# A recurrent attention and a two-layer product on one core: the order of all steps written anew

## The chip, the core and the metric

The kernel runs on one core of one Trainium2 chip. The core has five engines that run side by side, each through its own list of instructions in order: TensorE (PE, matmuls, with weight loads as a second track), VectorE (DVE), ScalarE (ACT), GpSimd (POOL) and SyncE (SP, which here only issues DMAs). Matmuls write to PSUM, from which DVE and ACT can read. The metric is the device time of one execution in microseconds (us), smaller is better. Differences are told against the median of the runs.

## The reference

For each of 4 batches and 8 heads (768 tokens, head size 48) a state matrix is carried through the tokens, and the result is put through two matrix products with a clipped quadratic between them:

```python
for t in range(S):
    cur = einsum('bhd,bhe->bhde', u * k[t], v[t])
    y[t] = einsum('bhd,bhde->bhe', r[t], state + cur)
    state = w * state + einsum('bhd,bhe->bhde', k[t], v[t])
x = y as (3072 tokens, 384)
h = x @ w_in                       # 384 -> 2048
g = where(h >= 1, h, where(h <= -1, 0, (h + 1)**2 / 4))
out = g @ w_out                    # 2048 -> 384, float32
```

## The kernel before

**Tiling.** Tokens are taken in chunks of 128. A *unit* is one chunk of one batch, a *group* is a chunk of two batches, so there are 12 groups (0 to 11) of two units each; group g has the units 2g and 2g+1. Groups 0 and 1 (the first chunk of all four batches) are worked unit by unit, the others mostly as whole groups. The hidden layer of a group is worked in four *quarters* of 512 columns.

**Steps.** Every step is a small function `do_<name>`, and a string `ORDER` lists all steps one after the other. Reading it from left to right gives each engine its list; nothing else sets the order. A word such as `m0.1/1` means step m of group 0, quarter 1, in PSUM place 1; `Ks1.0=G` means step Ks of group 1, unit 0, on engine G (GpSimd; V is VectorE, A is ScalarE). In a word like `M3.12` the two digits behind the point are unit 1 and quarter 2. The steps:

- `LK`, `LR`, `LV` load k, r and v through SP's queue (line 253); `WI0` to `WI2` and `WO0` to `WO2` load the two weight matrices in pieces through POOL's queue (lines 244, 247).
- `ln`, `bw`, `bu`, `wq` bring the logarithm of w (`lwp`) and u (`up`) to all partitions with matmuls (lines 207, 211, 233). `Wup`, `Wdn` put the powers of w in PSUM (tiles up_t, dn_t), `WupS`, `WdnS` in SBUF, `uS` copies u to SBUF, `wE` and `wC` make the decay over a whole chunk.
- `Rs`, `Ks` scale r and k by powers of w, `KU` and `RKU` form u*k and r*u*k, `us` sums the latter per head (line 304), `V` casts v to bf16, `B` multiplies v by those sums (all of line 282, 112, 313).
- `TR`, `TK`, `T` transpose the scaled r and k on TensorE (line 330), `cR`, `cK`, `c` copy them out; from group 4 on DMA transposes on SP do it (`RT`, `KT`, line 318).
- `A`, `AA` are the scores (line 370), `AT` masks them (lines 379, 384, always DVE), `Y` multiplies them by v and adds the state's part (lines 432, 438), `y`, `yg` add B (lines 446, 450, always DVE).
- `Sp`, `Tm`, `decayg`, `sbf` carry the state (lines 405, 409, 413, 416).
- `X` and `xc` transpose y on TensorE for groups 0 to 2; from group 3 on `xcg` does it with a DMA transpose on SP (line 467). The result is the tile xT.
- `m` is a quarter of the first product (line 475, 12 matmuls into the tile hp). The clipped quadratic takes three steps: `r` (line 486 on ACT, or a clamp in line 483 on DVE), `s` (lines 493, 495, ACT), `g` (line 498, always DVE, which also reads hp).
- `M` is one unit and quarter of the second product (line 512, 4 matmuls into the tile op), `og`, `o`, `oA`, `oB` copy the sums out, `stg`, `st`, `stA`, `stB` store them. Unit 1 of group 11 is worked in two halves of 192 columns.
- `Z` issues idle matmuls on a zero tile, whose result nobody reads (line 566).

**PSUM.** The eight banks form two pairs (places 0 and 1 of `pair`) and, in the opening, four single banks (places 0 to 3 of `bank`). With the first pair of place 2 or 3 the single banks are given up and become two more pairs. A step that writes a place waits until the last reader of what stood there is done. All idle matmuls write one tile in pair 0, made once at the start by `Zs`.

The lines that a sentence can't say are the loop that turns the list into instructions and the copy of the last unit's halves, which both read one tile:

```python
for word in ORDER.split():
    ...
    steps[kind](e, [int(x) for x in banks], *args)

def half_out(e, g, j, i):
    copy(e, make("o", ("o", g, j, i), [P, UNITS, DO], F32)[:, 0, : DO // 2], tiles["op", g, j][:, i, : DO // 2])
```

Of the kernel before, what the change touches and what calls it, by code (L numbers as in the profile page):

```python
# [9 lines left out]
F32 = mybir.dt.float32  # L10
# [8 lines left out]
FG = 4  # L19
# [5 lines left out]
Zs/0 ln Z19 bw/1 LK0.0 bu/0 uS=V LK1.0 LR0.0 LK0.1 LR0.1 LV0.0 wq/2 WdnS Ks1.0=G LR1.0 LR1.1 Wdn/3 Ks0.0=V Ks0.1=V  # L25
TK0/0 Wup/1 Rs0.0=V TR0/3 LK1.1 cK0=A WupS KU0.1=G KU0.0=V RKU0.0=G cR0=A KU1.0=G LV0.1 Rs0.1=V Z2 TR1/1 A0/03 LV1.0
LV1.1 WI0 WI1 WI2 us0.0 cR1=A TK1/1 cK1=A AT0.1 Z4 A1/13 Rs1.0=V LR2.0 LR2.1 Rs1.1=V V0.1 AT1.0 V0.0 Z9 TR3/1 B0.0=G
AT1.1 RKU0.1=V wE AT0.0 wC=A us0.1 Z7 Y1/3 TR2/0 B0.1=G Y0/2 y0 y1 cR2=A RKU1.0=G Z8 X0/2 Z4 TK2/3 X1/0 Ks1.1=G xc0=A
Sp1/2 cK2=A xc1=A Z7 TK3/3 cK3=A Tm1 A2/20 m0.0/0 cR3=V us1.0 AT2.1 AT2.0 r0.0=A A3/31 AT3.1 KU1.1=G RKU1.1=G m0.1/1
V1.0 s0.0=A B1.0=G Sp2/2 AT3.0 us1.1 r0.1=A Tm2 Y2/3 y2 g0.0 V1.1 X2/0 LK2.0 Y3/1 B1.1=G s0.1=A LK2.1 Sp0/2 Sp3/3  # L30
xc2=V LK3 y3 WO0 WO1 m0.3/0 r0.3=A s0.3=A g0.1 X3/1 Tm0 xc3=V m0.2/1 LR3 LV2.0 Tm3 m1.1/2 g0.3 r1.1=V m1.0/3 m1.2/0
Ks2=G r0.2=A s0.2=A g0.2 sbf2=A s1.1=A r1.0=A s1.0=A sbf3=A g1.1 m1.3/1 r1.2=V WO2 KU2=G LV2.1 M0.00/2 M0.10 M0.11
M0.01 g1.0 M1.00/3 M1.10 M1.11 M1.01 Rs2=G s1.2=A g1.2 T5/0 RKU2=G LK4 r1.3=A s1.3=A g1.3 T4/1 LV3 Ks3=G M0.02 M0.03
LR4 us2 c5=V A5/0 KU3=G Rs3=G c4=V A4/1 AT5 sbf1=A M1.02 M0.12 M0.13 AT4 T6/0 sbf0=A V2 Y4/1 Y5 B2=G og0=A T7/2 c6=A
RKU3=G c7=A yg2 LV5 M1.12 Sp4/0 Sp5 M1.03 X5/2 Tmg2 decayg2=G X4/1 M1.13 A6/0 xc4=A xc5=V m2.0/2 A7/1 us3 AT6 m2.1/0
og1=A LK5 LR5 V3 Y6/3 B3=G sbfg2=A r2.0=A AT7 Y7 m2.2/1 s2.0=A Ks4=G yg3 xcg3 m2.3/3 g2.0 Rs4=G r2.1=A s2.1=A g2.1 LV4
# [574 lines left out]
```

## Time and profile before

| | before |
|---|---|
| median of 3 runs | 173.95 us (173.92 to 174.29) |
| profiled execution: span from its first to its last instruction | 172.6 us |
| TensorE busy in it | 164.4 us, 1674 matmuls |
| VectorE, ScalarE, GpSimd busy in it | 130.6, 129.9, 117.4 us |
| first matmul of m0.0, of m0.2 | 19.21, 27.27 us from the span's start |
| end of the last matmul | 169.14 us |

The span is one profiled execution, from its first to its last instruction; what lies around it, about 1.35 us, is the difference to the median of the timed runs. In the groups of the profile a row gives source line, engine, operation, output and inputs, shape and count, then busy time and mean duration in ns, then the engine's idle time just before and who ended it. In the timeline a row gives start and length in us. Tile names carry no numbers there.

### The profile page before, as it was taken

To read this page: it belongs to the slowest core of one execution; us is meant where nothing else is said; L and a number is where in the kernel's file an instruction comes from. 1 tells how busy PE (TensorE), PEld (TensorE's weight loads), DVE (VectorE), ACT (ScalarE), POOL (GpSimd) and SP (SyncE) were. 2 spreads that over 40 slices of the span, in tenths; PEclk is the share of its full clock that TensorE was granted. 3 is DMA by queue.
4 is the path that set the end of the run, shared out by engine and by line. 5 is a ranking of instruction groups with operands and counts; after the bars stand their busy time and mean duration, and the time that the engine had idled before them with its cause. 6 is when DMAs were issued, how large, how long until landed. Compare 5 with 4: busy or idle time off the path is not lost.

```text
span 172.6 us, 4051 instructions
## 1 busy us (share of the span) xinstructions
PE 164.4 (95%) x1674; PEld 132.9 (77%) x1674; DVE 130.6 (76%) x150; ACT 129.9 (75%) x150; POOL 117.4 (68%) x86
## 2 busy tenths in 40 slices
PE   7989968999999999989999999999999999999991
PEld 5769868966889777588787797696897787888871
DVE  4578698988687688859789779885889959873752
ACT  4355698991699899189979879689695896988940
POOL 3496744998689949999999998999568804300000
PEclk9999999999999999999999999999999999999999
DMA  6999999998996999999999997998999025140022
GB/s 114 194 184 179 199 187 180 228 210 174 206 191 99 206 184 168 194 199 145 196 312 210 182 220 163 223 182 155 297 170 267 4 52 145 37 104 0 8 91 91
DMA packets 103751, 28.26 MB, mean 164 GB/s; under 512 B 98866, under 2 KB 102836, under 8 KB 103732
## 3 DMA queue, kind: packets, MB, share of 16 engines
q1 hardware_dynamic: 101824, 24.75, 79.9%
q0 software_dynamic: 1760, 3.15, 9.8%
q8 instruction: 13, 0.21, 0.6%
q10 hardware_dynamic: 148, 0.10, 0.2%
q14 instruction: 6, 0.05, 0.1%
HBM read 20.45 MB, written 4.72 MB: 146 GB/s over the span
## 4 chain that ended last, share of the span: by engine, by line
PE 87%; ACT 4%; DMA 2%; DVE 2%; issue 1%; POOL 0%; ACTq 0%; DVEq 0%
PE hp L475 35%; PE op L512 34%; PE A L370 4%; PE Y L438 3%; DMA xT<-y 2%; PE Y L432 2%; PE Sp L405 2%; PE z L566 2%; ACT pt L486 1%; PE T L330 1%; ACT TT L112 1%; PE lwp L207 1%; PE wp L233 1%; PE TR L330 1%; PE TK L330 1%
## 5 line engine op out<-in xcount | busy, mean ns | idle before, releaser
L475 PE MATMUL hp<-xT,w_in 128*128 128x256 bf16 x576 | 69.1, 273 | 1.3 <-DMA xT<-y 0.8
L512 PE MATMUL op<-w_out,g 128*128 128x384 bf16 (+1 forms) x400 | 68.4, 320 | 0.0
L498 DVE SCALAR_TENSOR_TENSOR g<-sq,hp 128x1024 bf16<-128x1024 bf16 x48 | 57.9, 1215 | 13.2 <-ACT sq L495 13.2
L475 PEld LDWEIGHTS <-w_in 128*128 128x128 bf16 x576 | 61.9, 114 | 4.6 <-issue 1.6
L486 ACT ACTIVATE pt<-hp 128x1024 f32<-128x1024 f32 x46 | 46.9, 1021 | 13.7 <-PE hp L475 13.7
L512 PEld LDWEIGHTS <-g 128*128 128x128 bf16 x400 | 37.5, 98 | 20.4
L495 ACT ACTIVATE sq<-pt 128x1024 bf16<-128x1024 f32 x46 | 48.3, 1057 | 1.2
L379 DVE TENSOR_TENSOR AT<-A,umask 128x1024 bf16<-128x1024 f32 x20 | 23.7, 1220 | 5.2 <-PE A L370 5.2
L282 POOL TENSOR_TENSOR Ks<-Ki,Wdn 128x768 bf16<-128x768 f32 (+1 forms) x12 | 20.3, 1689 | 8.5 <-ACT Wdn L225 3.4
L313 POOL TENSOR_TENSOR V<-Vb,diag 128x768 f32<-128x768 bf16 (+1 forms) x14 | 18.1, 1291 | 9.8 <-DVE diag L304 4.4
L282 POOL TENSOR_TENSOR RKU<-Ri,KU 128x768 f32<-128x768 f32 (+1 forms) x13 | 21.2, 1630 | 1.1 <-DVE KU L282 0.7
L282 POOL TENSOR_TENSOR KU<-Ki,u_sb 128x768 f32<-128x768 f32 (+1 forms) x13 | 21.2, 1634 | 0.4 <-DMA Ki<-in_k_dram 0.4
L416 POOL TENSOR_TENSOR state<-Tm,wCm 128x768 f32<-128x768 f32 x8 | 14.6, 1824 | 9.8 <-DVE Tm L413 9.8
L282 POOL TENSOR_TENSOR Rs<-Ri,Wup 128x768 bf16<-128x768 f32 x10 | 18.2, 1820 | 0.3 <-DMA Ri<-in_r_dram 0.3
L112 ACT CAST Vb<-Vi 128x768 bf16<-128x768 f32 (+1 forms) x14 | 10.2, 733 | 5.4 <-DMA Vi<-in_v_dram 5.4
L450 DVE TENSOR_TENSOR y<-Y,V 128x768 bf16<-128x768 f32 x10 | 9.6, 956 | 5.9 <-PE Y L438 3.3
L304 DVE TENSOR_REDUCE diag<-RKU 128x16 f32<-128x768 f32 (+1 forms) x14 | 11.6, 831 | 1.5 <-POOL RKU L282 1.5
L112 ACT CAST state_bf<-state 128x768 bf16<-128x768 f32 (+1 forms) x12 | 8.5, 717 | 4.4 <-POOL state L416 4.4
L112 ACT COPY o<-op 128x768 f32<-128x768 f32 (+1 forms) x9 | 6.7, 748 | 6.0 <-PE op L512 5.9
L438 PE MATMUL Y<-Vb,AT 128*128 128x48 bf16 x192 | 10.4, 186 | 0.4 <-ACT Vb L112 0.4
L438 PEld LDWEIGHTS <-AT 128*128 128x128 bf16 x192 | 9.5, 98 | 0.7 <-issue 0.5
L413 DVE TENSOR_TENSOR Tm<-Sp,state 128x768 f32<-128x768 f32 x8 | 7.7, 956 | 3.1 <-PE Sp L405 3.1
(73 smaller groups left out, 123.3 us busy)
## 6 DMA issues: line engine op xcount, KB each, us to landing
out_dram<-o SPq DMA_DIRECT2D x11, 384.0 KB, 3.8
Ki<-in_k_dram SPq DMA_DIRECT2D x9, 384.0 KB, 6.2
Ri<-in_r_dram SPq DMA_DIRECT2D x9, 384.0 KB, 6.2
Vi<-in_v_dram SPq DMA_DIRECT2D x9, 384.0 KB, 5.4
Ki<-in_k_dram SPq DMA_DIRECT2D x6, 192.0 KB, 4.0
Ri<-in_r_dram SPq DMA_DIRECT2D x6, 192.0 KB, 4.7
Vi<-in_v_dram SPq DMA_DIRECT2D x6, 192.0 KB, 6.0
w_in<-in_moe_w_in_dram POOLq DMA_DIRECT2D x2, 384.0 KB, 7.5
```

The source lines that it names most:

```text
L112: nc.scalar.copy(out, in_) if e == "A" else engines[e].tensor_copy(out, in_)
L282: engines[e].tensor_mul(part(out)[:, :, :, :D], part(a), rep(b, j1 - j0) if len(b.shape) == 3 and b.shape[1] == H else part(b))
L304: nc.vector.tensor_reduce(d[:, hs], tiles["RKU", g][:, hs, :], AX.X, ALU.add)
L313: engines[e].tensor_mul(t[:, hs, :], tiles["V", g][:, hs, :], tiles["diag", g][:, hs].unsqueeze(2).to_broadcast([P, n, D]))
L379: nc.vector.tensor_mul(t.rearrange("p i n t -> p (i n) t"), tiles["A", n].rearrange("p i (n t) -> p (i n) t", t=P), umask.unsqueeze(1).to_ ...
L416: engines[e].tensor_mul(states[g % BP], tiles["Tm", g], flat(wCm).unsqueeze(1).to_broadcast([P, UNITS, DM]))
L438: nc.tensor.matmul(Y[:, h * D : (h + 1) * D], AT[:, i, p, :], V[:, j * H + h, :], start=(c == 0), stop=True, skip_group_check=True,)
L475: nc.tensor.matmul(hp[:, f, :], w_in_sb[wi][:, i, wo * FG * P + f : (wo + 1) * FG * P : FG], tiles["xT", g][:, :, i, :], start=(i == 0), s ...
L486: nc.scalar.activation(t, tiles["hp", g, q], AF.Relu, bias=0.5, scale=0.5)
L495: nc.scalar.activation(t, p, AF.Square)
L498: nc.vector.scalar_tensor_tensor(out=make("g", ("g", g, q), [P, FG, TOK], BF16), in0=tiles["sq", g, q], scalar=1.0, in1=tiles["hp", g, q], ...
L512: nc.tensor.matmul(tiles[key][:, i, : o1 - o0], tiles["g", g, q][:, f, j * P : (j + 1) * P], w_out_sb[wi][:, wo, f * DO + o0 : f * DO + o1 ...
```

## The change

The string `ORDER` is replaced as a whole. No step is added to or taken from the mathematics; their sequence changes, some move to another engine, and idle matmuls stand in other places (67 instead of 60, in nine bursts instead of eight, the first of 9 instead of 19). Three small changes of code go with it. An idle burst now takes a PSUM tile of its own (`Z` a single bank in the opening, `Zp` a pair). Each half of the last unit gets its own tile, so that a half's copy waits for that half alone, and which of its four quarters comes first is counted instead of fixed. `V` may run on another engine than ACT.

What moves between engines: to DVE two more KU, two more RKU (and two of half size), one Ks, one B, two decays, five more clamps `r`, half of a V cast, two half transposed copies and one whole; to POOL another half V cast; to ACT two more output copies of a group and the one of the last group's unit 0.

The diff, cut to its core (of `ORDER` two lines):

```diff
 ORDER = """
-Zs/0 ln Z19 bw/1 LK0.0 bu/0 uS=V LK1.0 LR0.0 LK0.1 LR0.1 LV0.0 wq/2 WdnS Ks1.0=G LR1.0 LR1.1 Wdn/3 Ks0.0=V Ks0.1=V
...
+ln=A LK1.1 LR0.0 LK0.0 Z9/0 bu/3 LK0.1 bw/1 Wup=A/0 Wdn=A/0 uS=V Rs0.0=V LR0.1 LK1.0 wq/3 Ks0.0=V LV0.0 LR1.1 KU0.1=V
...
     def do_V(e, b, g, j=None):
...
-        copy("A", t[:, hs, :], tiles["V32", g][:, hs, :])
+        copy(e or "A", t[:, hs, :], tiles["V32", g][:, hs, :])
...
-        key = ("op", g, j) if last else ("op", g)
-        if key not in tiles:
-            tiles[key] = pair(b[0], F32, "op")
         wi, wo = part(q, OUT_PARTS)
         for i, o0, o1 in [(i, i * DO // 2, (i + 1) * DO // 2) for i in halves] if last and j else [(j, 0, DO)]:
+            key = ("op", g, j, i) if last else ("op", g)
+            if key not in tiles:
+                tiles[key] = pair(b.pop(0), F32, "op")
+            n = counts["op", g, j, i] = counts.get(("op", g, j, i), 0) + 1
             for f in range(FG):
                 nc.tensor.matmul(
...
-                    start=(q == 0 and f == 0), stop=(q == nQ - 1 and f == FG - 1),
+                    start=(n == 1 and f == 0), stop=(n == nQ and f == FG - 1),
...
-        copy(e, make("o", ("o", g, j, i), [P, UNITS, DO], F32)[:, 0, : DO // 2], tiles["op", g, j][:, i, : DO // 2])
+        copy(e, make("o", ("o", g, j, i), [P, UNITS, DO], F32)[:, 0, : DO // 2], tiles["op", g, j, i][:, i, : DO // 2])
...
-    def do_Zs(e, b):
-        tiles["z"] = pair(b[0], F32, "z")
+    def idling(t, n):
+        for i in range(n):
+            nc.tensor.matmul(t, idle[:, :P], idle[:, :P], start=True, stop=True)
 
     def do_Z(e, b, n):
-        for i in range(n):
-            nc.tensor.matmul(tiles["z"][:, 0, :P], idle[:, :P], idle[:, :P], start=True, stop=True)
+        idling(pair(b[0], F32, "z")[:, 0, :P] if later else bank(b[0], [P, P], F32, "z"), n)
+
+    def do_Zp(e, b, n):
+        idling(pair(b[0], F32, "z")[:, 0, :P], n)
```

On DVE, from the first mask of group 1 to the second y of that group, the list before was this (AT_401 and AT_416 are the masked scores of units 3 and 2, state is the first state of a batch, y_458 the y tile of group 1):

```order
L384 TENSOR_TENSOR AT_401<-A1_376,umask_105 128x512
L384 TENSOR_TENSOR AT_401<-A0_375,umask_105 128x512
L384 TENSOR_TENSOR AT_416<-A1_407,umask_105 128x512
L384 TENSOR_TENSOR AT_416<-A0_406,umask_105 128x512
L304 TENSOR_REDUCE diag_399<-RKU_323 128x8
L409 TENSOR_TENSOR state_123<-Sp_439,wCm_110 128x384
L446 TENSOR_TENSOR y_458<-Y_449,V2_437 128x384
L498 SCALAR_TENSOR_TENSOR g_460<-sq_435,hp_385 128x1024
L112 COPY xT_492<-X_463 128x384
L446 TENSOR_TENSOR y_458<-Y_469,V2_437 128x384
```

And in the change (the two y of group 1 go to y_460):

```order
L387 TENSOR_TENSOR AT_387<-A1_356,umask_105 128x512
L387 TENSOR_TENSOR AT_387<-A0_355,umask_105 128x512
L285 TENSOR_TENSOR RKU_336<-Ri_166,KU_173 128x384
L387 TENSOR_TENSOR AT_427<-A0_391,umask_105 128x512
L412 TENSOR_TENSOR state_122<-Sp_401,wCm_110 128x384
L307 TENSOR_REDUCE diag_383<-RKU_336 128x8
L387 TENSOR_TENSOR AT_427<-A1_392,umask_105 128x512
L501 SCALAR_TENSOR_TENSOR g_458<-sq_412,hp_367 128x1024
L449 TENSOR_TENSOR y_460<-Y_432,V2_408 128x384
L115 CAST Vb_406<-Vi_259 128x384
L501 SCALAR_TENSOR_TENSOR g_466<-sq_464,hp_414 128x1024
L449 TENSOR_TENSOR y_460<-Y_495,V2_408 128x384
```

The second y now has a product RKU, a cast of half of V1 and a second g ahead of it; one transposed copy has moved behind it.

On POOL, the pieces of the first weight matrix stood together before, behind the first four products:

```order
L282 TENSOR_TENSOR Ks_91<-Ki_156,Wdn_114 128x8x48
L282 TENSOR_TENSOR KU_195<-Ki_151,u_sb_115 128x384
L282 TENSOR_TENSOR RKU_198<-Ri_158,KU_195 128x384
L282 TENSOR_TENSOR KU_201<-Ki_156,u_sb_115 128x384
L244 DMA w_in0_116<-in_moe_w_in_dram 128x3x512
L244 DMA w_in1_117<-in_moe_w_in_dram 128x3x512
L244 DMA w_in2_118<-in_moe_w_in_dram 128x3x1024
```

In the change:

```order
L285 TENSOR_TENSOR RKU_176<-Ri_131,KU_168 128x384
L247 DMA w_in0_116<-in_moe_w_in_dram 128x3x512
L285 TENSOR_TENSOR Ks_92<-Ki_129,Wdn_114 128x8x48
L247 DMA w_in1_117<-in_moe_w_in_dram 128x3x512
L285 TENSOR_TENSOR Ks_92<-Ki_129,Wdn_114 128x8x48
L316 TENSOR_TENSOR V2_280<-Vb_226,diag_183 128x384
L285 TENSOR_TENSOR KU_173<-Ki_129,u_sb_115 128x384
L316 TENSOR_TENSOR V2_280<-Vb_226,diag_183 128x384
L247 DMA w_in2_118<-in_moe_w_in_dram 128x3x1024
L115 CAST Vb_406<-Vi_259 128x384
```

w_in0 now comes behind three products, with a scaling of k between it and w_in1, and w_in2 behind four more steps.

On SP, what stands ahead of the first DMA transpose of y (group 3), before:

```order
L253 DMA Ki_677<-in_k_dram 128x16x48
L253 DMA Vi_694<-in_v_dram 128x16x48
L253 DMA Ri_705<-in_r_dram 128x16x48
L253 DMA Vi_809<-in_v_dram 128x16x48
L253 DMA Ki_896<-in_k_dram 128x16x48
L253 DMA Ri_898<-in_r_dram 128x16x48
L467 DMA_TRANSPOSE xT_952<-y_950 128x6x128
```

and in the change:

```order
L256 DMA Vi_658<-in_v_dram 128x16x48
L256 DMA Vi_693<-in_v_dram 128x16x48
L256 DMA Ri_695<-in_r_dram 128x16x48
L256 DMA Ki_697<-in_k_dram 128x16x48
L256 DMA Ri_699<-in_r_dram 128x16x48
L256 DMA Ki_701<-in_k_dram 128x16x48
L470 DMA_TRANSPOSE xT_962<-y_956 128x6x128
```

The six loads (k and r of groups 4 and 5, v of groups 3 and 4) are the same, in another sequence.

76 lines of the change are left out of this document (38 added, 38 removed).

## The prediction

> **What bounds the kernel now.** I read the page first: busy shares, the chain that ended last, the costliest groups.
>
> ```profile
> PE 164.4 (95%) x1674; PEld 132.9 (77%) x1674; DVE 130.6 (76%) x150; ACT 129.9 (75%) x150; POOL 117.4 (68%) x86
> ...
> PEclk9999999999999999999999999999999999999999
> ...
> PE 87%; ACT 4%; DMA 2%; DVE 2%; issue 1%; POOL 0%; ACTq 0%; DVEq 0%
> ...
> L498 DVE SCALAR_TENSOR_TENSOR g<-sq,hp 128x1024 bf16<-128x1024 bf16 x48 | 57.9, 1215 | 13.2 <-ACT sq L495 13.2
> L486 ACT ACTIVATE pt<-hp 128x1024 f32<-128x1024 f32 x46 | 46.9, 1021 | 13.7 <-PE hp L475 13.7
> L495 ACT ACTIVATE sq<-pt 128x1024 bf16<-128x1024 f32 x46 | 48.3, 1057 | 1.2
> ...
> Ki<-in_k_dram SPq DMA_DIRECT2D x6, 192.0 KB, 4.0
> ```
>
> TensorE is busy for 95% of the span and carries 87% of the chain, while DVE, ACT and POOL each have a quarter or more in hand. A quarter of the hidden layer costs 1.02 us (r) + 1.06 (s) + 1.22 (g) = 3.30 us behind its matmuls. Next, TensorE's waits, and two pieces of the chain in order of time (start, length, work).
>
> ```profile
> PE X L460 <- DVE y L446: 1.0, 1, 1.0
> PE hp L475 <- DMA xT<-y: 0.8, 1, 0.8
> PE hp L475 <- DVE g L498: 0.5, 1, 0.5
> PE Y L438 <- ACT Vb L112: 0.4, 1, 0.4
> ...
> 57.76 1.31 PE hp L475 x12
> 59.07 0.65 PE op L512 x4
> ...
> 68.81 0.96 DVE y L450
> 69.80 4.27 DMA xT<-y
> ```
>
> All waits but one lie before 27.3 us. The one behind is m4.0, which stands 0.8 us for its transposed input. From 27.27 us to the last matmul TensorE otherwise has work without a gap: a quarter (12 matmuls) takes 1.31 us, a step of the second product 0.65. Both kernels issue the same such work behind m0.2, and no idle burst stands there, so the order can gain in three places only: up to m0.2, at the 0.8 us, and after the last matmul.
>
> **The opening, up to the first quarter m0.0.** Times of the changed kernel are from here on my walk through its lists, with durations of these rows.
>
> ```profile
> 3.44 1.64 PE L207 MATMUL lwp<-lnw,ones 1*128 1x384 f32 x2 [0.24 <-ACT lnw L203]
> ...
> 4.88 1.48 PE L211 MATMUL up<-u_row,ones 1*128 1x384 f32 x2
> ...
> 7.80 0.61 PE L330 MATMUL TK<-ident,Ks 128*128 128x128 bf16 x4
> ...
> 10.08 0.61 PE L370 MATMUL A<-TT 48*128 48x128 bf16 x8
> ...
> 15.87 1.03 PE L566 MATMUL z<-idle 128*128 128x128 bf16 x8
> ...
> 16.15 1.02 DVE L446 TENSOR_TENSOR y<-Y,V 128x384 bf16<-128x384 f32 x2 [0.61 <-PE Y L438]
> ...
> 18.00 0.55 PE L566 MATMUL z<-idle 128*128 128x128 bf16 x7
> ...
> 19.21 1.50 PE L475 MATMUL hp<-xT,w_in 128*128 128x256 bf16 x12
> ```
>
> The up product now goes first. When u_row lands has no row; up ran at 4.88 straight behind lwp, so it was there by then. If it is there at 3.1 us (an estimate, a little before lwp's own start), up ends near 4.8 and lwp, which needs 1.3 us more, near 6.1 instead of 5.1. The exponentials move 1.0 us later, the copy of u into SBUF, which follows up (6.36 before), 1.5 us earlier. DVE now has Rs0.0 before Ks0.0, so Ks0.0 ends at 7.7 and TK0 starts at 7.8, as before: the swap costs nothing there. TR0 then stands behind four idle matmuls and needs PSUM bank 0, which holds dn_t until Ks0.1 has read it (8.7); A0 starts near 10.6 against 10.08. The two masks of unit 1 are done at 14.65, y0 at 15.15, y1 at 16.5 (before: both at 17.2), since DVE has fewer products of the later group in between. But X1, eight idle matmuls, TR2 and A3 stand ahead of m0.0 on TensorE: 17.05 + 0.35 + 0.8 + 0.45 + 0.45 gives m0.0 at 19.1. Against 19.21 that is no gain. Idle matmuls cost 0.13 us each at 15.9 us (1.03 for eight) and 0.08 at 18.0 (0.55 for seven, with the end of the last; some 0.06 from one start to the next), while the granted clock is 9 tenths or more in every slice. So with fast ones m0.0 comes at 18.7; with 0.5 us less luck at u_row and bank 0 it is 19.6. I take 19.1.
>
> **From m0.0 to m0.2.** This is the main term. DVE's list from the first mask of group 1 on, before:
>
> ```profile
> 19.53 1.28 DVE L384 TENSOR_TENSOR AT<-A,umask 128x512 bf16<-128x512 f32 x2
> 21.11 1.29 DVE L384 TENSOR_TENSOR AT<-A,umask 128x512 bf16<-128x512 f32 x2 [0.30 <-PE A L370]
> ...
> 22.78 0.55 DVE L409 TENSOR_TENSOR state<-Sp,wCm 128x384 f32<-128x384 f32 x1
> ...
> 23.73 1.21 DVE L498 SCALAR_TENSOR_TENSOR g<-sq,hp 128x1024 bf16<-128x1024 bf16 x1
> ...
> 25.53 0.56 DVE L446 TENSOR_TENSOR y<-Y,V 128x384 bf16<-128x384 f32 x1 [0.32 <-POOL V L313]
> 26.00 1.21 DVE L498 SCALAR_TENSOR_TENSOR g<-sq,hp 128x1024 bf16<-128x1024 bf16 x1
> ```
>
> The second y of group 1 ends at 26.1, with one g ahead of it. In the change a product RKU1.0, a cast of half of V1 and the second g stand ahead of it too. From 19.15 (A3 done): four masks 2.6, RKU1.0 0.5, state and reduction 1.0, g0.0 1.15, y 0.5, the cast 0.45, g0.1 1.15, y 0.55, total 7.9: the second y ends at 27.05, 0.95 later. (Each costs about 0.07 less than its row says, because the next begins before it ends. The cast of 128x384 on DVE has no row; it lies between the 0.35 of DVE's xT copy and the 0.56 of its f32 copy of u.)
>
> TensorE beside it, before:
>
> ```profile
> 22.54 0.36 PE L438 MATMUL Y<-Vb,AT 128*128 128x48 bf16 x8
> 23.87 0.34 PE L460 MATMUL X<-ident,y 128*128 128x128 bf16 x3 [0.97 <-DVE y L446]
> 24.64 0.36 PE L438 MATMUL Y<-Vb,AT 128*128 128x48 bf16 x8 [0.42 <-ACT Vb L112]
> 25.18 1.47 PE L475 MATMUL hp<-xT,w_in 128*128 128x256 bf16 x12
> 26.48 0.33 PE L460 MATMUL X<-ident,y 128*128 128x128 bf16 x3
> 27.27 6.73 PE L475 MATMUL hp<-xT,w_in 128*128 128x256 bf16 x60 [0.45 <-DVE g L498]
> ```
>
> From the first Y of group 1 to m0.2 that is 4.73 us, of which 1.84 are waits. In the change m0.1 ends at 22.75 and Y3 follows at 22.85; then come 9 idle matmuls (0.55), Sp3 (0.35), 22 idle ones (1.3), X3 0.3, Y2 0.35, m0.3 1.35, X2 0.3, Sp2 and Sp1 0.55: 5.45 us with Y3 itself. The 31 idle matmuls take the 1.85 us that were waits; the rest grew because Sp1, Sp2, Sp3 now lie here. m0.2 starts at 28.3 instead of 27.27: **+1.0 us**. The ends: idle matmuls at 0.13 us each add 2.1 (m0.2 at 30.4); an early m0.0 at 18.0 takes 1.1 off (27.2).
>
> **Loads and weights.** Two landings from the view of DMA issues (microseconds from issue to landing):
>
> ```profile
> Vi<-in_v_dram SPq DMA_DIRECT2D x1, 192.0 KB, 11.0
> ...
> w_in<-in_moe_w_in_dram POOLq DMA_DIRECT2D x1, 768.0 KB, 12.6
> ```
>
> While the three w_in transfers run, a 192 KB load takes 11 us; the median of the K halves on the page is 4.0. POOL now issues w_in0 near 9.3 us instead of 10.8, so the twelfth load, half of V1, lands near 24.9, just when DVE's cast wants it (24.95), and the eleventh near 21.8, in time for POOL's cast (1.0, as POOL's other 384-wide steps) and Y3. I cost both at nothing; the cover is a few tenths.
>
> **Behind m0.2.** DVE receives five clamps, two KU, two RKU, one Ks, one B, two decays and some copies, and gives up two output copies.
>
> ```profile
> L483 DVE TENSOR_SCALAR pt<-hp 128x1024 f32<-128x1024 f32 x2 | 2.4, 1220 | 0.0
> ```
>
> Five times 1.22, eight times 0.96 (the y row, same size) and 1.1 of smaller work: about 15 us, so DVE goes to 146 of 172.6 us. TensorE's list covers it: the shortest stretch between a quarter and the first user of its g or its PSUM pair is 3.7 us in both orders (a quarter 1.31, a mask product 0.55, a Y pair 0.75 and steps of 0.65), against the chain of 3.30. It costs nothing unless something queues ahead of r, s or g; both ends are priced below. Group 3's transposed load has the same six loads ahead of it on SP as before. For m4.0 the work between the last Y and the quarter grows from 4.45 to 4.79 us (two Sp more); need was 0.96 + 4.27 + 0.1. But g3.2 now stands directly ahead of that y on DVE, behind r3.2, a state copy and s3.2 on ACT, and I get the y 0.3 us later. I leave the 0.8 as it is; the ends are 0 and 1.2.
>
> **The tail.**
>
> ```profile
> 169.14 0.32 ACT L112 COPY o<-op 128x192 f32<-128x192 f32 x1 [3.13 <-PE op L512]
> 169.49 0.36 DVE L112 COPY o<-op 128x192 f32<-128x192 f32 x1 [0.45 <-ACT o L112]
> ```
>
> The two half copies came one after the other because they read one tile. With tiles of their own, the DVE half, now finished first on TensorE, is copied 0.35 us before the other half ends. But all three last stores now stand on SP, 0.34 us of issue each: the last issue ends about 1.05 us after the last matmul in both. Zero, between -0.3 and +0.2.
>
> **Sum.** Against the profiled span of 172.6: 0 (opening) + 1.0 (to m0.2) + 0 + 0 = 173.6. The median of the runs, 173.95, is 1.35 above that span, so the forecast is **174.9 us**, slower by 0.5%. Its own range is 174.3 to 175.8.
>
> **Rivals.** (a) *TensorE turns fast early.* If the idle matmuls between the opening's transposes bring it to the fast rate by about 11 us instead of 17, the 23 idle matmuls and five transposes between A0 and m0.0 cost half, m0.0 starts near 18.0 (when xT is there), and the 9.05 us of list behind it give m0.2 at 27.05: -0.2. If the y of group 4 is then on time too, the longer cover takes another 0.35: 173.4, faster. For it: idle matmuls now also lie between TK0, TR0 and A0. Against it: the opening burst shrinks from 19 to 9, and an idle matmul still took 0.13 us at 15.87, although the list of waits holds none above 1.0 us. The Trainium skill (TensorE: Matmul & The Clock Gate, Part 1) says that the array runs at half rate until about 3.4 us of sustained work; by that rule the changed opening is fast from 8 us and this rival's time follows, but the trace of before disagrees, being slow at 15.87. Chance 0.27.
>
> (b) *Half of V1 lands late.* If the w_in transfers hold their share without a gap, the twelfth load lands at 26.3 to 27.6; DVE's cast waits, and g0.1 and the second y with it, one for one beyond 24.95: 176.3 at the nearer end. Chance 0.13.
>
> (c) *DVE becomes the bound behind m0.2.* If the moved products stand ahead of g where only 0.4 us are spare (3.7 against 3.3), each such place costs some 0.3; six of the twelve groups make 1.8: 176.7. Against it: DVE's share stays at 85%. Chance 0.08.
>
> (d) *Nothing moves.* The walk's terms cancel and m0.2 starts where it did: 174.0. Chance 0.14.
>
> The forecast has 0.38. A difference under 0.2% (0.35 us) can't be told from none. Faster: 0.27, from (a). Same: 0.16, (d) and the low edge of the forecast. Slower: 0.57. The range runs from 172.9 (half a microsecond below (a)) to 177.0, above (c).
>
> **What would show it.** Right: first matmul of TK0 at 7.8, m0.0 near 19, the second y of group 1 behind both g's at about 27, an unbroken hp stretch from about 28.3, and the wait of m4.0 still near 0.8. Wrong: idle matmuls at 0.06 us before 12 us and the stretch before 27.3 (rival a); DVE waiting for a DMA before its cast (b); new TensorE waits on g or AT behind 28 us (c); a last store that ends more than 0.3 us nearer to the last matmul.

## The result

The change makes the kernel slower: the median is 176.69 us (four executions, 176.55 to 176.81) against 174.12 us of the kernel before in the same comparison, a ratio of 1.0133 (95% interval 1.0105 to 1.0162; the quotient of the two medians is 1.0148). Ratios here and below leave out executions that lie over 1.5% above the fastest of the same kernel. Forecast were 174.9 us, with 172.9 to 177.0 as range and 0.57 for slower. The sign held, and the time lies in the whole range, though above the 174.3 to 175.8 of the forecast itself. The reason did not hold: the forecast's one term, a microsecond between m0.0 and m0.2, did not come, and two places that it priced at nothing cost the time.

From here on lines of the changed kernel are the lines before plus 3. The page of the changed kernel, its first part and its clock row:

```profile
PE 165.3 (95%) x1681; PEld 132.7 (76%) x1681; DVE 147.8 (85%) x166; ACT 124.6 (71%) x143; POOL 103.8 (59%) x77
...
PEclk9999999999999999999999999999999999999999
```

DVE's share is where the forecast had it (146 us). TensorE's waits in the profiled execution:

```profile
PE Y L441 <- DVE AT L387: 2.6, 1, 2.6
PE up L214 <- DMA u_row<-in_u_dram: 1.0, 1, 1.0
PE z L566 <- DVE idle L137: 1.0, 1, 1.0
PE hp L478 <- DVE AT L382: 0.7, 1, 0.7
```

Two of these are new behind the start: 2.6 us for masks before Y0, and 0.7 us for masks before a quarter of the hidden layer. The 0.8 us for m4.0's transposed load is gone. Where the masks were late stands in the timeline of the changed kernel (start, length, engine, line, work):

```profile
8.41 1.00 POOL L285 TENSOR_TENSOR RKU<-Ri,KU 128x384 f32<-128x384 f32 x1 [1.02 <-DMA Ri<-in_r_dram]
8.55 1.28 DVE L285 TENSOR_TENSOR RKU<-Ri,KU 128x384 f32<-128x384 f32 x1
...
11.72 2.57 DVE L285 TENSOR_TENSOR Rs<-Ri,Wup 128x384 bf16<-128x384 f32 x1
12.07 1.01 POOL L285 TENSOR_TENSOR Ks<-Ki,Wdn 128x384 bf16<-128x384 f32 x1
13.03 0.83 POOL L316 TENSOR_TENSOR V<-Vb,diag 128x384 f32<-128x384 bf16 x1
13.81 1.32 POOL L285 TENSOR_TENSOR KU<-Ki,u_sb 128x384 f32<-128x384 f32 x1
14.67 1.87 DVE L387 TENSOR_TENSOR AT<-A,umask 128x512 bf16<-128x512 f32 x3
15.40 0.50 PE L441 MATMUL Y<-Vb,AT 128*128 128x48 bf16 x8 [2.58 <-DVE AT L387]
...
18.64 1.06 PE L566 MATMUL z<-idle 128*128 128x128 bf16 x8
...
20.60 1.50 PE L478 MATMUL hp<-xT,w_in 128*128 128x256 bf16 x12
...
28.71 1.47 PE L478 MATMUL hp<-xT,w_in 128*128 128x256 bf16 x12
...
109.23 1.80 POOL L285 TENSOR_TENSOR Ks<-Ki,Wdn 128x768 bf16<-128x768 f32 x1
109.49 2.36 DVE L285 TENSOR_TENSOR RKU<-Ri,KU 128x768 f32<-128x768 f32 x1
112.64 2.34 DVE L382 TENSOR_TENSOR AT<-A,umask 128x1024 bf16<-128x1024 f32 x2
113.90 1.47 PE L478 MATMUL hp<-xT,w_in 128*128 128x256 bf16 x12 [0.72 <-DVE AT L382]
```

A product of 128x384 costs DVE 0.55 us. Rs1.1 took 2.57, and it ended 0.43 us behind the end of POOL's B0.0 (13.86 to 14.29). RKU0.0 took 1.28 and ended 0.42 us behind POOL's RKU0.1 (9.41). RKU9, of 128x768, took 2.36 instead of 0.95 and ended 0.82 behind POOL's Ks9. All three read both of their inputs from SBUF, and each ends behind a POOL step by about its own running time. Before, DVE had four such steps, and none began while a POOL product ran. In the change it has fourteen. Five of them met a POOL product and took longer than others of their size: these three (Rs1.1 began 0.35 us ahead of the product that went first), B3 at 53.01 (1.40) and KU11 at 126.09 (1.30). A sixth, at 61.40, began 0.03 us before a product's end and took 0.95. The groups of Rs1.0 and Rs1.1 show it as well, before and after:

```profile
L282 DVE TENSOR_TENSOR Rs<-Ri,Wup 128x384 bf16<-128x384 f32 x2 | 1.0, 550 | 0.0
...
L285 DVE TENSOR_TENSOR Rs<-Ri,Wup 128x384 bf16<-128x384 f32 x2 | 3.1, 1559 | 0.0
```

Where the span's 2.3 us (172.6 to 174.9) lie:

| from to | before | after | difference |
|---|---|---|---|
| start to m0.0 | 19.21 | 20.60 | +1.39 |
| m0.0 to m0.2 | 8.06 | 8.11 | +0.05 |
| m0.2 to the start of m11.3 | 135.12 | 135.87 | +0.75 |
| m11.3 to the end of the span | 10.19 | 10.29 | +0.10 |

Outside the span nothing changed. The four executions of the changed kernel have 1.75 to 1.81 us there, and the 67 of the kernel before that were timed beside the experiments have 1.72 to 1.85. The 1.35 us of the forecast came from setting the median time against the span of an execution that was longer than the median one.

### The profile page after: what moved, and what is told of

It reads as the page before. It is cut to its first block, busy times and chain, and to the rows that moved or that the text cites. A ratio compares the mean times of both kernels' runs of the same rounds, so it can differ in the third digit from the quotient of the medians.

```text
span 174.9 us, 4046 instructions
## 1 busy us (share of the span) xinstructions
PE 165.3 (95%) x1681; PEld 132.7 (76%) x1681; DVE 147.8 (85%) x166; ACT 124.6 (71%) x143; POOL 103.8 (59%) x77
## 5 line engine op out<-in xcount | busy, mean ns | idle before, releaser
L489 ACT ACTIVATE pt<-hp 128x1024 f32<-128x1024 f32 x41 | 41.9, 1021 | 18.7 <-PE hp L478 17.6
L498 ACT ACTIVATE sq<-pt 128x1024 bf16<-128x1024 f32 x41 | 43.3, 1058 | 1.2
L316 POOL TENSOR_TENSOR V<-Vb,diag 128x768 f32<-128x768 bf16 (+1 forms) x13 | 16.6, 1276 | 25.6 <-ACT Vb L115 11.1
L285 POOL TENSOR_TENSOR KU<-Ki,u_sb 128x768 f32<-128x768 f32 (+1 forms) x11 | 18.6, 1691 | 3.2 <-DVE u_sb L115 3.1
L285 POOL TENSOR_TENSOR Ks<-Ki,Wdn 128x768 bf16<-128x768 f32 (+1 forms) x11 | 18.4, 1677 | 1.3 <-PE Sp L408 1.2
L285 POOL TENSOR_TENSOR RKU<-Ri,KU 128x768 f32<-128x768 f32 (+1 forms) x9 | 16.3, 1814 | 1.0 <-DMA Ri<-in_r_dram 1.0
L115 ACT COPY o<-op 128x768 f32<-128x768 f32 (+2 forms) x12 | 8.7, 728 | 8.7 <-PE op L515 8.7
L419 POOL TENSOR_TENSOR state<-Tm,wCm 128x768 f32<-128x768 f32 x6 | 11.0, 1830 | 5.7 <-DVE Tm L416 5.7
L441 PE MATMUL Y<-Vb,AT 128*128 128x48 bf16 x192 | 10.6, 186 | 2.6 <-DVE AT L387 2.6
L496 ACT ACTIVATE sq<-pt 128x1024 bf16<-128x1024 f32 x7 | 7.4, 1055 | 3.0 <-DVE pt L486 3.0
L115 ACT CAST Vb<-Vi 128x768 bf16<-128x768 f32 (+1 forms) x12 | 9.1, 773 | 0.5 <-DMA Vi<-in_v_dram 0.5
```

The costliest lines, as they stand in the source:

```text
L115: nc.scalar.copy(out, in_) if e == "A" else engines[e].tensor_copy(out, in_)
L285: engines[e].tensor_mul(part(out)[:, :, :, :D], part(a), rep(b, j1 - j0) if len(b.shape) == 3 and b.shape[1] == H else part(b))
L316: engines[e].tensor_mul(t[:, hs, :], tiles["V", g][:, hs, :], tiles["diag", g][:, hs].unsqueeze(2).to_broadcast([P, n, D]))
L441: nc.tensor.matmul(Y[:, h * D : (h + 1) * D], AT[:, i, p, :], V[:, j * H + h, :], start=(c == 0), stop=True, skip_group_check=True,)
L489: nc.scalar.activation(t, tiles["hp", g, q], AF.Relu, bias=0.5, scale=0.5)
L498: nc.scalar.activation(t, p, AF.Square)
```

## The experiments

Theory (*port*): a DVE step with two SBUF inputs that meets a running POOL product stands still till POOL is done, and the loss follows from three such meetings. The Trainium skill has this as a rule (SBUF — State Buffer, Who interferes with whom): such a step and a POOL instruction that reads SBUF share one read interface, and the one that comes second is blocked for the whole of the other. Rivals: late data; the list behind m0.0; the loads.

**Rs1.1 from PSUM.** The same values stand in the PSUM tile up_t, so one input can come from there with the order unchanged.

```diff
-        t = tiles["up_t"] if g == 0 and "up_t" in tiles else flat(Wup)
+        t = tiles["up_t"] if (g == 0 or (g, j) == (1, 1)) and "up_t" in tiles else flat(Wup)
```

> The changed kernel, in which Rs1.1 alone reads the powers of w from the PSUM tile up_t instead of from the SBUF tile Wup (the same values; order and all else stay). Theory (port): a DVE step with two SBUF inputs that meets a running POOL product stands still until that product ends; with one input in PSUM it does not. Rs1.1 then takes 0.55 us instead of 2.57 and ends near 12.3, Y0's wait of 2.6 us falls below 1.0, y0 ends near 15.2 instead of 17.0, and m0.0 starts at 18.6 to 19.3 instead of 20.60, since POOL's B0.1 and the transposes stand behind it still. m0.2 then starts near 27.3 instead of 28.71, and the time is 175.0 to 175.6 us. Rival (late data): Rs1.1 stood because r of unit 3 was not there; then it ends at 14.3 again and the time stays at 176.7. Rival (idle matmuls or DVE's list behind m0.0 set m0.2): Rs1.1 gets short, but m0.2 stays at 28.3 or later, and the time at 176.2 to 176.7.

One execution took 175.28 us, the other three 183.71 to 185.65; the profiled one is of the long kind. Its timeline:

```profile
11.96 0.55 DVE L285 TENSOR_TENSOR Rs<-Ri,up_t 128x384 bf16<-128x384 f32 x1
...
18.67 1.50 PE L478 MATMUL hp<-xT,w_in 128*128 128x256 bf16 x12
...
26.80 3.40 PE L478 MATMUL hp<-xT,w_in 128*128 128x256 bf16 x29
...
50.91 1.82 POOL L285 TENSOR_TENSOR Ks<-Ki,Wdn 128x768 bf16<-128x768 f32 x1
51.18 9.42 DVE L316 TENSOR_TENSOR V<-Vb,diag 128x768 f32<-128x768 bf16 x1
...
57.99 1.79 POOL L285 TENSOR_TENSOR Ks<-Ki,Wdn 128x768 bf16<-128x768 f32 x1
...
61.72 2.72 PE L478 MATMUL hp<-xT,w_in 128*128 128x256 bf16 x12 [7.96 <-DVE y L453]
```

Rs1.1 took 0.55 us, m0.0 came at 18.67 and m0.2 at 26.80, 1.9 us sooner: late data and the list behind m0.0 fall as causes of that loss. RKU0.0 still met POOL and took 1.11 us, so its meeting is not what held m0.0. The port theory is borne out for Rs1.1 by an edit that moved one operand and nothing else. What nobody expected is B3, the product that the change had moved to DVE: it met five POOL products in a row and stood till the last of them was over (59.78; it ended 0.82 later, 9.42 us in all). TensorE waited 7.96 us for it. In the profiled execution of the changed kernel the same B3 came 0.6 us before the end of one product, was let in behind it, and took 1.40.

**RKU9 on POOL.**

```diff
-RKU9=V
+RKU9=G
```

> The changed kernel, with RKU9 back on POOL (the place in the list stays). Theory (port): RKU9 on DVE (109.49, 2.36 us) makes two masks of group 8 late, and they alone cause the 0.72 us in which TensorE waits before m7.0 (113.90); without it that wait goes, 176.0 us, give or take 0.2. Rival: POOL gets 1.8 us more ahead of Ks9 and B8, so that y of group 8 and its transposed load come late and a wait takes the place of the one removed: 176.5 to 177.0.

175.29 us, ratio 1.0079 (1.0040 to 1.0117). Five of the eight executions took 174.85 to 175.44, three 176.25 to 176.91, about as long as the changed kernel. In the profiled one (175.15) the 0.72 us wait is gone; m7.0 there:

```profile
112.68 1.47 PE L478 MATMUL hp<-xT,w_in 128*128 128x256 bf16 x12
```

From m0.2 to m11.3 it took 134.69 instead of 135.87. The two traces agree to 0.02 us from m0.2 to m7.1 and from m7.3 to m11.3; between m7.1 (108.41 in the changed kernel) and m7.3 it took 8.31 instead of 9.47, so RKU9 on DVE cost 1.2 us, more than the one wait that the list shows for it, while KU11, further down, ran in 0.95 instead of 1.30 without any gain. The edit takes the whole product off DVE, not its stall alone; but at 0.95 us the first mask would have ended near 112.5, before m7.0 was due at 113.2 (an estimate from the rows of the changed kernel). The rival (a late B8) falls for this execution; what made three executions longer is open.

**Both edits**, as the two diffs above show them.

> Both edits at once. Theory (port): they add, since one lies before 28 us and one at 110: 174.2 to 174.9 us. If all of the loss against the kernel before came from steps that stood still beside POOL, it is within 0.3 us of 174.1. Rival: the list behind m0.0 (idle matmuls, second g and product ahead of the second y) costs its 1.0 us as the prediction has it; then it is 175 or more.

The executions took 173.56 and 173.74; 175.05 to 175.34 (three); 183.41 to 185.48 (five); none lies in the expected 174.2 to 174.9. Without the last group the ratio is 1.0015 (0.9982 to 1.0047). The profiled one (173.74), one of the two short ones, has m0.0 at 18.50, m0.2 at 26.82, m11.3 at 161.71 and a span of 172.0: 2.9 us less than the change, 0.6 less than before. In it the two edits take away more than the whole loss in the span; the rival, the list's 1.0 us, falls.

**The cost by itself.** A tail behind the kernel before runs DVE steps alone and beside POOL products:

```diff
+    def pool_products(n):
+        for i in range(n):
+            nc.gpsimd.tensor_mul(gb, ga, ga)
+    def two_sbuf():
+        for i in range(6):
+            nc.vector.tensor_mul(dx, flat(Wup), flat(u_sb))
...
+    two_sbuf()
...
+    pool_products(4)
+    two_sbuf()
...
+    pool_products(4)
+    for i in range(6):
+        nc.vector.tensor_add(dx, ps, flat(u_sb))
...
+    pool_products(4)
+    for i in range(6):
+        nc.vector.tensor_copy(db, flat(u_sb))
...
+    for i in range(3):
+        nc.gpsimd.dma_start(out=w_in_sb[0], in_=w_in_src[:, :, : FG * P])
+    two_sbuf()
```

> The kernel before, with a tail behind its last copy that measures the disputed cost by itself: six DVE steps of 128x384 at a time, alone or beside four POOL products of 128x768 (f32, 1.8 us each). Theory (port): six DVE products with two SBUF inputs take 2.9 us alone (0.48 each); beside POOL each waits for the POOL product that runs, so the six take 7 us or more, and POOL's products also get longer by about 0.5 each. Six DVE additions with one PSUM input stay at 2.9 beside POOL. Beside three DMA issues on POOL the two-input products stay at 2.9. Rival (POOL slows all that DVE does): the additions with a PSUM input get longer too. The six plain casts from f32 to bf16 (one SBUF input, 0.35 each) aren't decided by the theory as told; with them short, the number of SBUF inputs is what counts.

One step of each part, in that order, and for the second part also two of POOL's products:

```profile
172.38 0.56 DVE L604 TENSOR_TENSOR Wdn<-Wup,u_sb 128x384 f32<-128x384 f32 x1
...
184.26 1.66 POOL L600 TENSOR_TENSOR state<-state 128x768 f32<-128x768 f32 x1
184.62 1.70 DVE L604 TENSOR_TENSOR Wdn<-Wup,u_sb 128x384 f32<-128x384 f32 x1
185.99 1.66 POOL L600 TENSOR_TENSOR state<-state 128x768 f32<-128x768 f32 x1
...
191.53 0.56 DVE L616 TENSOR_TENSOR Wdn<-ps,u_sb 128x384 f32<-128x384 f32 x1
...
199.46 1.51 DVE L620 CAST state_bf<-u_sb 128x384 bf16<-128x384 f32 x1
...
205.38 3.52 DVE L604 TENSOR_TENSOR Wdn<-Wup,u_sb 128x384 f32<-128x384 f32 x6
```

Two SBUF inputs: 0.56 alone, 1.70 beside POOL, whose products took 1.66 there instead of 1.47. One input in PSUM: 0.56 beside POOL. Beside DMA issues: six in 3.52, as alone (3.52); only the first of the three issues ran at the same time. The open point came out against "two inputs alone count": a plain cast within SBUF, 0.36 alone, took 1.51. The Trainium skill (same page and section) names casts among the steps that can take both interfaces; this trace agrees. The rival (POOL slows all that DVE does) falls with the PSUM row.

**B3 on POOL too.**

```diff
-B3=V
+B3=G
```

> The changed kernel with three edits: Rs1.1 reads up_t in PSUM, RKU9 is back on POOL, and B3 is back on POOL (its place in the list stays). With the first two alone the time fell into groups (173.6 to 173.7, 175.1 to 175.3 and 183.4 to 185.5 us), and in a traced execution of the long kind B3 on DVE took 9.42 us, over five POOL products in a row (51.18 to 60.60). Theory (port): which group comes depends only on whether B3 gets its turn behind the first, or only behind the last of these five products; with B3 on POOL the groups are gone and every time is 173.4 to 174.0 us, 0.2 to 0.5 below the kernel before. Rival (another cause, for instance the granted clock or the loads): times above 175 come again. Rival: POOL, 1.5 us longer in front of Rs4, makes y of group 3 and its transposed load late: one group, but 174.3 or more.

174.05 us (173.45 to 175.15), ratio 0.9987 (0.9962 to 1.0013). None of ten executions is above 175.2, and none of the 52 of the later kernels with this edit is above 176.4: the 183 to 186 us were B3's. The rest of the expectation fails: three of ten still lie at 174.77 to 175.15, so B3 was not the only cause of spread, and the ratio's interval contains 1: with three edits the new order is as fast as the old one, not faster.

**Rs1.0 ahead of RKU1.1**, on top of the three edits.

```diff
-RKU1.1=V Rs1.0=V
+Rs1.0=V RKU1.1=V
```

> The same with Rs1.0 ahead of RKU1.1 on DVE. In the trace with two edits the two stood beside POOL's cast of half of V1 (0.79 and 0.85 us instead of 0.55), and TensorE waited 0.67 us before the transposes TR2, which need Rs1.0. Theory (port, and the opening sets m0.2): that wait falls below 0.2, m0.0 starts near 18.0 instead of 18.5, m0.2 near 26.3, and the time is 0.3 to 0.6 us below that of the kernel with three edits: 172.9 to 173.6. Rival (the loads or the second y set m0.2): m0.2 stays at 26.8 and the time is the same within 0.2.

174.06 us, ratio 0.9996 (0.9966 to 1.0026): the rival is right. m0.0 stands at 18.53 (18.66 with three edits) and m0.2 at 26.81 (26.77). The wait of 0.67 us that the edit was to remove is not in the trace with three edits either.

**Without the 31 idle matmuls** Z9 and Z22, on top of the three edits.

```diff
-Y3/2 Z9/1 Sp3/3
+Y3/2 Sp3/3
...
-Z22/0 X3/1
+X3/1
```

> The kernel with three edits without the 31 idle matmuls between Y3 and X3 (Z9 and Z22). The step of the prediction that put m0.2 one microsecond later rests on DVE's list, with these idle matmuls only in the place of waits. Theory (that step): TensorE waits there for y instead; m0.2 and the time stay as in the kernel with three edits within 0.2 us. Rival (they stand in the way): the time falls by 0.3 or more. Rival (they keep TensorE at its fast rate): the matmuls behind them get slow (X3 near 0.5 instead of 0.34, the quarter m0.3 above 1.5), and the time grows by 0.3 or more.

175.31 us, ratio 1.0067 (1.0043 to 1.0092), with two executions at 173.58 and 173.72 and six at 175.19 to 176.04. The profiled one is of 173.72:

```profile
24.15 0.34 PE L463 MATMUL X<-ident,y 128*128 128x128 bf16 x3 [1.25 <-DVE y L449]
24.42 0.37 PE L441 MATMUL Y<-Vb,AT 128*128 128x48 bf16 x8
24.97 1.50 PE L478 MATMUL hp<-xT,w_in 128*128 128x256 bf16 x12 [0.18 <-DMA w_in<-in_moe_w_in_dram]
```

X3 waits for y instead and runs at the fast rate (0.34), and m0.2 starts at 26.81: in this execution idle matmuls neither cost nor give anything there. The quarter m0.3 waits 0.18 us for w_in2, so a load stands close behind. The times don't bear the first theory out: most executions are about 1.5 us longer, and why this trace can't say.

**The load of w_in2 sooner**, on top of the three edits.

```diff
-B0.0=G TR3/2 KU1.0=G B0.1=G y0=V WI2
+B0.0=G TR3/2 B0.1=G WI2 KU1.0=G y0=V
```

> The changed kernel with Rs1.1 from PSUM, RKU9 and B3 on POOL, and three neighbours on POOL in another order: B0.0, B0.1, the load of w_in2, KU1.0 instead of B0.0, KU1.0, B0.1, w_in2. In the traces with three edits the load of w_in2 was issued at 15.6 to 15.8 and landed 9.1 to 9.2 us later, at 24.9, where the quarter m0.3 stood at 24.85 to 24.97, with a wait of 0.18 for that load in one of them; and y1 waited for POOL's B0.1. Theory (loads): with the stalls beside POOL gone, w_in2 sets m0.3 and with it m0.2. Issued near 14.4 it lands near 23.6; y1 ends 0.3 to 0.6 earlier, m0.0 starts near 18.1, m0.3 near 24.3, m0.2 near 26.2, and the time is 173.0 to 173.5 us, 0.4 to 0.7% below the kernel before. If the times of 174.8 to 175.5, which came in 3 of 10 and 6 of 8 executions, are those in which w_in2 lands later, they become rare. Rival (the second y of group 1 sets m0.2): within 0.2 us of the kernel with three edits.

174.16 us, ratio 0.9999 (0.9975 to 1.0023). In the profiled execution (174.10) the load was issued 1.0 us sooner than with three edits (14.65 instead of 15.64) but landed only 0.3 sooner, m0.2 came 0.11 sooner (26.66), and the gain went in two places:

```profile
15.48 1.01 POOL L285 TENSOR_TENSOR KU<-Ki,u_sb 128x384 f32<-128x384 f32 x1
16.19 1.17 DVE L285 TENSOR_TENSOR RKU<-Ri,KU 128x384 f32<-128x384 f32 x1
16.43 0.50 POOL L115 CAST Vb<-Vi 128x384 bf16<-128x384 f32 x1
...
38.96 1.46 PE L515 MATMUL op<-w_out,g 128*128 128x384 bf16 x8 [0.49 <-DMA w_out<-in_moe_w_out_dram]
```

KU1.0, now later on POOL, holds up RKU1.1, which also has to let POOL's cast pass (m0.0 stays at 18.54), and TensorE now waits 0.49 for a piece of w_out.

**The last stores apart**, on top of that.

```diff
-st11.0 stA11.1 stB11.1
+st11.0 stB11.1 stA11.1=A
```

> The same, and at the end the last half's store on ACT's queue and behind the other half's, which is ready first. In the trace with three edits the halves were copied by 168.32 and 168.60, and SP issued both stores from 168.63 on, 0.85 us together. Expected: the last issue ends 0.3 to 0.5 us sooner, and the time is 0.2 to 0.5 us lower than with the four edits. Rival (the landing of the last store counts from its copy, and the queue is not the limit): the same time within 0.1.

174.33 us, ratio 1.0001 (0.9981 to 1.0021). From m11.3 to the end of the span it took 10.20 us against 10.26: the rival is right, the queue is not the limit. But the profiled execution is a long one (175.58), and it shows one way in which an execution gets long. Its timeline:

```profile
123.89 1.82 POOL L285 TENSOR_TENSOR RKU<-Ri,KU 128x768 f32<-128x768 f32 x1
123.95 2.57 DVE L285 TENSOR_TENSOR KU<-Ki,u_sb 128x768 f32<-128x768 f32 x1
...
127.71 2.78 PE L478 MATMUL hp<-xT,w_in 128*128 128x256 bf16 x24 [1.16 <-DVE g L501]
```

The same place with three edits (173.59 us):

```profile
123.31 1.04 DVE L285 TENSOR_TENSOR KU<-Ki,u_sb 128x768 f32<-128x768 f32 x1
...
123.49 2.55 POOL L285 TENSOR_TENSOR RKU<-Ri,KU 128x768 f32<-128x768 f32 x1
```

KU11 on DVE and RKU10 on POOL meet. With three edits KU11 begins 0.18 us ahead of RKU10, while POOL's Rs10 still runs (to 123.52); it is let in behind Rs10 and ends in 1.04, and RKU10 is the one that stands (2.55 instead of 1.82), which TensorE doesn't wait for. In the long execution KU11 begins 0.06 us behind RKU10 and takes 2.57, g comes late, and TensorE waits 1.16.

**The order with four edits, without idle matmuls**: w_in2 sooner, the old stores, and Z9 and Z22 taken out by the diff shown for them above.

> The four edits, without the 31 idle matmuls Z9 and Z22. With three edits the kernel without them had the same m0.2 (26.81 against 26.77), but 6 of 8 executions took 175.2 to 176.0 us instead of 173.6 to 173.7. Theory (late w_in2): w_in2 issued 1.2 us sooner takes these away, and the times are those of the kernel with four edits, within 0.2. Rival (idle matmuls hold something up that the traced executions didn't show, such as the granted clock): most executions again take 1.5 us more than the shortest.

174.79 us (173.37 to 176.36), ratio 1.0008 (0.9972 to 1.0044): w_in2 was not the cause of the long executions. Six of ten took 174.7 or more, about as the rival has it, against two of the twelve with the idle matmuls; with three edits it was six of eight against three of ten. So kernels without these idle matmuls are long more often, and no run shows why. The profiled one, 174.87, has KU11 at 2.05 us and a wait of 0.6 for g. So of six profiled executions with B3 on POOL the four at 173.6 to 174.1 have KU11 at 0.95 to 1.04, and the two at 174.9 and 175.6 have it at 2.05 and 2.57. That KU11 makes the spread is read from these six traces and not shown; the kernel with KU11 on POOL as well, which should show it and should lie near 173.6 in every execution, was not tried.

**When is DVE let in?** Two tails of eight trials each: POOL does five products in a row, DVE one product of 128x768, which comes 0 to 7 short copies later.

```diff
+    for n in range(8):
...
+        for o in outs:
+            nc.gpsimd.tensor_mul(o, ins, dve_in[0])
+        for i in range(n):
+            nc.vector.tensor_copy(small[:, :144], ps[:, :144])
+        nc.vector.tensor_mul(dve_out, dve_in[0], dve_in[1])
```

In the second tail the five products are Ks, KU, Rs, KU, Ks, and DVE's is B.

> The kernel before, with a tail behind its last copy: eight times POOL does five independent products of 128x768 (f32, 1.8 us each) in a row, and DVE one product of the same size with two SBUF inputs, which comes 0, 1, 2, ... 7 short copies (one PSUM input, about 0.22 us each) after POOL's first has begun. The question is what decides whether DVE gets its turn behind the first POOL product or only behind the last. Theory (late comers win): in the traces DVE won where it came 0.5 to 0.7 us before the end of a POOL product (rows 53.01, 126.09) and lost over five where it came 1.55 us before it (51.18); then the first trials last 8 us or more and those that come in the last 0.7 us last 1.4 to 1.7. Rival (turn by turn, as the repeated short products showed: 1.61 to 1.71 each): no trial lasts longer than one POOL product and its own 0.95, 2.8 us.

> The kernel before, with a tail behind its last copy: the eight trials again, with the very kinds of step that met in group 2: on POOL Ks, KU, Rs, KU, Ks (128x768, Rs and Ks to bf16 in rows of 64), on DVE the product B (v in bf16 times one number per head). With plain f32 products DVE got its turn behind the first POOL product in each of eight trials (0.95 to 2.46 us), which the theory that late comers win did not expect. Theory (the kind of step decides): some trials last over two or more POOL products, 4 us or more, above all those that begin early in the first. Rival (turn by turn always, and the 9.42 us of B3 had another cause): all eight last at most 2.8 us.

First, sixth and seventh trial with plain products, then of the second tail with the kinds of step of group 2:

```profile
173.07 2.46 DVE L609 TENSOR_TENSOR V<-Vi 128x768 f32<-128x768 f32 x1
...
224.63 0.95 DVE L609 TENSOR_TENSOR V<-Vi 128x768 f32<-128x768 f32 x1
...
235.04 2.30 DVE L609 TENSOR_TENSOR V<-Vi 128x768 f32<-128x768 f32 x1
```

```profile
174.10 2.46 DVE L617 TENSOR_TENSOR V<-Vb,diag 128x768 f32<-128x768 bf16 x1
...
225.69 0.95 DVE L617 TENSOR_TENSOR V<-Vb,diag 128x768 f32<-128x768 bf16 x1
...
236.10 2.30 DVE L617 TENSOR_TENSOR V<-Vb,diag 128x768 f32<-128x768 bf16 x1
```

In all sixteen trials DVE was let in behind the POOL product that ran: it never took more than 2.46 us. So neither theory of what keeps it out longer (its time of arrival, the kind of step) is borne out. The trials leave two things out: TensorE and ACT had nothing to do in the tails, and no trial began ahead of POOL's first product, as Rs1.1 did. What let two POOL steps pass Rs1.1 and five pass B3 stays open.

## Why the prediction was right, and where it was wrong

**The opening, put at 0: wrong by 1.4 us.** "m0.0 at 19.1" came at 20.60. The failed step is one duration: Rs1.1 at 0.55, the mean of its row before, in a place where POOL runs. TK0 (7.8 forecast, 7.75) held, A0 came sooner than forecast (10.15 instead of 10.6), and RKU0.0's 1.28 us cost TensorE a wait of 0.18 us there; the masks of unit 1 were due at 14.65 and were done at 16.54. With Rs1.1's input in PSUM they were done at 14.76, y0 at 15.23 (forecast 15.15), and m0.0 stood at 18.67. The walk itself was right to 0.4 us. The row of before had no meeting in it, and so no price for one.

**From m0.0 to m0.2, put at +1.0: wrong.** The walk has 9.2 us between the two, 8.11 were measured, and 8.06 before. TensorE's list from Y3 to m0.2 was walked at 5.45 and took 4.85; Y3 came 3.26 behind m0.0 instead of 3.75; and DVE's second y ended 7.54 behind m0.0's start, not 7.95. The short steps Y, Sp and X of TensorE's list were priced at 2.25 us together and took 1.36 from one start to the next, because the next begins before they end; the idle matmuls and the quarter took 0.29 more than forecast. That the idle matmuls stand in the place of waits was right (m0.2 at 26.81 without them, 26.77 with).

**Loads, put at 0: right for the change.** No step waited for half of V1. With the stalls gone one trace shows a wait for w_in2, of 0.18 us.

**Behind m0.2, put at 0: wrong by 0.75, the sum of larger parts.** The 0.8 us of m4.0, left as it was, went away, and RKU9 cost 1.2; some 0.4 is left that stands in no wait. One product took 2.36 us instead of the 0.96 that it was priced at. The delay came as in rival (c), from a moved product in DVE's list, but ahead of masks and not of g, and not because DVE was full. That (c)'s price was 176.7 is chance.

The 0.8 us is no fixed part of the old order's time. Four traces have that order: the kernel before and the three with a tail. In two of them m4.0 waits for its transposed load (0.84 and 0.92 us), in two it doesn't. On SP, with the wait (the kernel before) and without it (the first trials):

```profile
68.98 0.57 SPq L253 DMA_DIRECT2D Ki<-in_k_dram  x1
69.80 2.10 SPq L467 DMA_TRANSPOSE xT<-y  x1
...
68.06 0.57 SPq L253 DMA_DIRECT2D Ki<-in_k_dram  x1
69.73 1.21 SPq L467 DMA_TRANSPOSE xT<-y  x1
```

Where the load of k began 0.7 to 0.8 us ahead, the transpose took 2.1 us to issue and landed after 4.3; where it began 1.6 to 1.7 us ahead, the transpose took 1.2 to 1.3 and landed after 3.0 to 3.1. In the change a load of v stands there, 3.0 us ahead, and the transpose landed after 2.8; none of the ten traces of the new order has the wait. That the distance to the load decides is read from these rows; no run tests it.

**The tail, put at 0 (-0.3 to +0.2): +0.10.** Tiles of their own let the two halves be copied side by side, and nothing was gained at the end.

**Outside the span, taken as 1.35: mis-sized.** It is 1.80 in the profiled execution, and 1.7 to 1.9 with either order. A span of 172.6 belongs to an execution of about 174.35 us, so the walk's 173.6 should have given 175.4.

**Rivals.** (a) falls: eight idle matmuls at 18.64 us took 1.06, the slow rate, in the changed kernel. With Rs1.1 from PSUM they were fast in five traces (0.61 to 0.64) and slow in three (1.06), and m0.0 came at 18.42 to 18.71 and at 18.53 to 18.67: their rate doesn't set it. (Its 9.05 us from m0.0 to m0.2 are 9.2 in the walk.) (b) falls: DVE's cast at 26.19 waited for no load. (d) falls with the time. The sum came out in the whole range by luck: a term of 1.0 that hardly came (0.05) was replaced by two that were not in it (1.39 and 0.75), the time outside the span added 0.45, and the range reached 177.0 only to hold (c). The prediction has no term for a meeting of DVE and POOL. The rule of the Trainium skill told above, applied to the new order's fourteen DVE steps, would have named places to look at, five of which met a POOL product.

## What to carry to other kernels

Before moving an elementwise product between DVE and GpSimd, list for each DVE step with two SBUF inputs, and each cast within SBUF, what POOL does at that time; its row's mean holds only where the two did not meet, and the loser's wait stands inside its own duration, not in the idle time before it, so compare the means of one form in both kernels. A step whose result TensorE soon needs should read one input from PSUM, or stay out of a stretch in which POOL has products in a row. Where such a meeting is decided by a tenth of a microsecond, the kernel's time can fall into groups, and one profiled execution shows only one of them. A forecast that adds a span and a time outside it should take both from the same execution.

## What was not expected of the hardware

- A DVE product of 128x768 stood 9.42 us beside five POOL products in a row, one of 128x384 stood 2.57 us over two, and RKU1.1 1.17 us over a product and a cast; in sixteen trials made for it none stood longer than one POOL product. The Trainium skill (SBUF — State Buffer, Who interferes with whom) has the blocked one wait for the instruction that holds the interface; these three waited longer than that.
- The blocking goes both ways: POOL's next product took 2.52 to 2.58 us instead of 1.80 when DVE was let in ahead of it.
- Rs1.1 began 0.35 us before POOL's Ks1.0 by the timeline (11.72 and 12.07), and still POOL went first. Before, two such products, at 11.34 and 11.80, took 0.55 each beside POOL's DMA issues. Starts on the two engines are not a safe sign of who holds what.
